# Attention scores of a head pair issued as one group, with two of their banks from the general PSUM pool

## The chip, the cores and the metric

The kernel runs on one NeuronCore of a Trainium2 chip, as one launch. The metric is the device time in microseconds of a whole execution. The median over 8 runs of the kernel before is 347.16 us (345.54 to 348.53).

A word on the engines as they are named here: PE is TensorE (PEld its weight loads), ACT is ScalarE, DVE is VectorE, POOL is GpSimd, SP is SyncE, which only issues transfers. [...]

## The reference

```python
def _attn_ref(q, k, v, f):                     # q, k, v: 8 x 8 x 576 x 64; f: 8 x 8 x 576
    scores = scale * np.matmul(q, k.transpose(0, 1, 3, 2))
    cum = np.cumsum(np.log(np.clip(f, 0.0001, 1.0)), axis=-1)
    decay = cum[:, :, :, None] - cum[:, :, None, :]
    scores = np.where(causal, -1000000000.0, scores + decay)
    attn = np.exp(scores - np.max(scores, axis=-1, keepdims=True))
    attn = attn / (np.sum(attn, axis=-1, keepdims=True) + 1e-09)
    return np.matmul(attn, v)

def _moe_ref(x, w_in, w_out):                  # x: 4608 x 512, w_in: 512 x 2048, w_out: 2048 x 512
    h = x @ w_in
    g = h * (1.0 / (1.0 + np.exp(-h)))
    return g @ w_out
```

The output of a causal attention with forgetting, 8 batches of 8 heads of 576 positions, its heads put side by side, goes through a two-layer block with SiLU (called MoE in the code). Inputs and output are float32.

## The kernel before

**Attention.** The first 128 positions of each batch are done ahead of the loop by other functions. The loop works on the other 448 positions, two heads at a time: a *pair* `n`, 32 of them, four to a batch. The decay is folded into the values (`convert_v` on POOL), so a probability is the exponential of the scaled score.

`scores(n, c)` does one of three chunks of a pair's scores (L445). The two heads lie in partitions 0 to 63 and 64 to 127, so each matmul uses 64 rows of PE, and the two heads' matmuls run beside each other, each into its own PSUM bank. A chunk gets a tile of two banks from the pool `psc` (two tiles, four banks). Chunk 0 holds the diagonal blocks, whose upper triangle DVE clears (L469). Chunk 1 holds the scores against the first key block. Chunk 2 holds what is left, and the rows of the last 64 queries. Chunks 0 and 1 take one exponential of 1024 columns each on ACT (L464), chunk 2 one of 256 (L464) and one of 640 (L476), whose last block DVE masks (L483).

`attend(n)` multiplies the probabilities with the values (28 small matmuls, `dn`, L507 and L516) and divides by the sum (L524, L525). `back(m)` turns the result of two pairs into the layout of the MoE input, on PE into a tile `tx` (L549) or, where `BY_DMA`, with two transposing transfers on SP's queue (L539, L543).

**MoE.** The rows of the MoE input come in 13 groups of up to 512 columns. `m1_chunk` makes one of 16 chunks of the hidden layer: four matmuls into a bank `hp` (L568), tanh on ACT (L576), and a multiply on DVE (L577) that reads `hp` again and writes `gt`. `m2_part` makes a quarter of an output tile: four matmuls into a bank `po` (L613), which stays open over four parts; after the fourth ACT copies it out (L623), and POOL's queue stores it later (L592).

**Banks.** The other four PSUM banks are the pool `pbig`. `hp`, `po`, `dn` and `tx` all take theirs from it, one at a time, in the order in which the program gave them back. A bank is given back by the last instruction that reads it: for `hp` the multiply on DVE.

**Order.** The order on every engine is the one in which the Python code emits instructions. `fill(us)` emits MoE pieces worth so many microseconds by a simple cost (columns / 2.4 ns), choosing between `m1_chunk` and `m2_part` in `step` so that the two keep pace. `slot(us, first)` calls `fill` and then issues the stores that were waiting. `behind()` is the MoE work that is ready and not yet emitted. The loop over `m` (two pairs each) is:

```python
        scores(n, 0)
        scores(n, 1)
        prepare(n)
        slot(piece, 2)
        # back(m - 1)
        scores(n, 2)
        scores(n + 1, 0)
        prepare(n + 1)
        slot(piece, 2)
        scores(n + 1, 1)
        scores(n + 1, 2)
        slot(piece, 2)
        attend(n)
        attend(n + 1)
        slot(min(3.5, max(0.8, behind() - LAG)) if m > 1 else 0.8, 1)
```

`prepare(n)` casts the q and k of pair `n + 2` on POOL, transposes them into `qkT` with a transfer on SP (L428), loads those of pair `n + 4`, and at some `n` loads and converts values of the next batch. After the loop only MoE work is left, some 59 us of it by `behind()`.

Of the kernel before, what the change touches and what calls it, by code (L numbers as in the profile page):

```python
# [8 lines left out]
ACT = mybir.ActivationFunctionType  # L9
ALU = mybir.AluOpType  # L10
FP32 = mybir.dt.float32
BF16 = mybir.dt.bfloat16
P = 128
# [5 lines left out]
def kernel(  # L19
# [10 lines left out]
    nc = tc.nc  # L30

    B, H, S, D = q.shape
# [5 lines left out]
    SM = 512  # L38
    ST = S - SM
    NM = SM // P  # L40
    NR = NM - 1
    RB = NR * P
# [9 lines left out]
    scale = 1.0 / float(D) ** 0.5  # L52
# [380 lines left out]
    T0 = P  # L433
# [8 lines left out]
    AT |= {(c, 0): SM + (c - 1) * P for c in range(1, NM)}  # L442
    AT |= {(2, 1): RB, (3, 1): SM + RB, (3, 2): 2 * SM}

    def scores(n, c):  # L445
        b, p = divmod(n, NP)
        if c == 0:
            us[n] = upool.tile([P, 2, UW], BF16, name="u", tag="u")
        u, ut = us[n], uts[n % 4]
        t = qkT[n]  # L450
        sc = psc.tile([P, 2, SM], FP32, name="sc", tag="sc")
        for kb, q0, q1, o in CHUNKS[c]:
            for i in range(2):
                r = slice(i * D, (i + 1) * D)
                if kb == 0:
                    kt = kT0[b][r, p, :]
                else:
                    k0 = RB if kb == NM else kb * P + RB
                    kt = t[r, k0 : k0 + P]
                nc.tensor.matmul(  # L460
                    sc[:, i, o : o + q1 - q0], lhsT=kt, rhs=t[r, q0:q1], start=True, stop=True
                )
        w = SM if c < 2 else T0
        nc.scalar.activation(  # L464
            out=u[:, :, c * SM : c * SM + w], in_=sc[:, :, 0:w], func=ACT.Exp, scale=scale
        )
        if c == 0:
            x = u[:, :, 0:RB].rearrange("p i (a t) -> p i a t", t=P)
            nc.vector.tensor_tensor(  # L469
                out=x,  # L470
                in0=x,
                in1=tri[:, None, None, :].to_broadcast([P, 2, NR, P]),
                op=ALU.mult,
            )
        if c == 2:
            nc.scalar.activation(  # L476
                out=ut[:, :, 0:3:2, :].rearrange("p k i t -> p i k t"),
                in_=sc[:, :, T0 : T0 + (NM + 1) * ST].rearrange("p i (k t) -> p i k t", t=ST),
                func=ACT.Exp,
                scale=scale,  # L480
            )
            x = ut[:, NM, 0:3:2, :]
            nc.vector.tensor_tensor(  # L483
                out=x, in0=x, in1=trit[:, None, :].to_broadcast([P, 2, ST]), op=ALU.mult
            )

    NGR = 2 * NR + 1

# [2 lines left out]
    def attend(n):  # L491
        b, p = divmod(n, NP)
        if p % 2 == 0:
            xqs[n // 2] = xqp.tile([P, NGR, 2, D], BF16, name="xr", tag="xr", bufs=3)
        xq = xqs[n // 2]
        u, ut = us.pop(n), uts[n % 4]
        dn = pbig.tile([P, NGR, D + 1], FP32, name="dn", tag="big")

        def vals(kb, i):
            h = head(p, i)  # L500
            return v0[b][:, h, :] if kb == 0 else vbf[b][:, kb - 1, h, :]

        for i in range(2):
            for c in range(1, NM):
                for kb in range(c + 1):
                    o = AT[c, kb]
                    nc.tensor.matmul(  # L507
                        dn[:, i * NR + c - 1, :],
                        lhsT=u[:, i, o : o + P],
                        rhs=vals(kb, i),  # L510
                        start=(kb == 0),
                        stop=(kb == c),
                    )
        for i in range(2):
            for kb in range(NM + 1):
                nc.tensor.matmul(  # L516
                    dn[:, NGR - 1, :],
                    lhsT=ut[:, kb, i : i + 2, :].rearrange("p i t -> p (i t)"),
                    rhs=vals(kb, i),
                    start=(i == 0 and kb == 0),  # L520
                    stop=(i == 1 and kb == NM),
                )
        rec = recp.tile([P, NGR], FP32, name="rec", tag="rec")
        nc.vector.reciprocal(out=rec[:, :], in_=dn[:, :, D])  # L524
        nc.vector.tensor_tensor(  # L525
            out=xq[:, :, p % 2, :],
            in0=dn[:, :, 0:D],
            in1=rec[:, :, None].to_broadcast([P, NGR, D]),
            op=ALU.mult,
        )  # L530
# [30 lines left out]
    def m1_chunk(g, fc):  # L561
        w = GW[g]
        if fc == 0:
            gts[g] = gpool.tile([P, NFC, w], BF16, name="gt", tag="gt")
        gt = gts[g]
        hp = pbig.tile([P, w], FP32, name="hp", tag="big")
        for cc in range(NCC):
            nc.tensor.matmul(  # L568
                hp[:, :],
                lhsT=w_in_bf[:, cc, fc * P : (fc + 1) * P],  # L570
                rhs=xcols(g, cc),
                start=(cc == 0),
                stop=(cc == NCC - 1),
            )
        th = tpool.tile([P, w], BF16, name="th", tag="th")
        nc.scalar.activation(out=th[:, :], in_=hp[:, :], func=ACT.Tanh, scale=0.5)  # L576
        nc.vector.scalar_tensor_tensor(  # L577
            out=gt[:, fc, :],
            in0=th[:, :],
            scalar=1.0,  # L580
            in1=hp[:, :],
            op0=ALU.add,
            op1=ALU.mult,
        )
# [4 lines left out]
    def store(n):  # L589
        n = max(n, 0)  # L590
        for q_, dst, src in stores[:n]:
            q_.dma_start(out=dst, in_=src)  # L592
        del stores[:n]
# [46 lines left out]
    def step():  # L640

        a, c = at["m1"], at["m2"]
        can1 = a < len(M1) and M1[a][0] in ready
        g1 = M1[a][0] if a < len(M1) else NG
        g2 = M2[c][0] if c < len(M2) else NG
        if can1 and M1[a][1] == 0 and g1 > g2 + 1:
            can1 = False
        can2 = open2["w"] and c < len(M2) and g2 < g1
        if not can1 and not can2:
            return None  # L650
        if can1 and can2:
            f1 = M1[a][1] / NFC
            f2 = (c - sum(M2_OF[:g2])) / M2_OF[g2]
            want = 3 - at["last"] if abs(f1 - f2) < 0.15 else (1 if f1 < f2 else 2)
            if want == at["last"] and at["row"] >= 2 and abs(f1 - f2) < 0.25:
                want = 3 - want
            if sum(M2_OF[: g2 + 1]) - c <= 2 and f1 >= 0.75:
                want = 1
            can1 = want == 1
        kind = 1 if can1 else 2  # L660
        at["row"] = at["row"] + 1 if kind == at["last"] else 1
        at["last"] = kind
        if can1:
            m1_chunk(*M1[a])
            at["m1"] += 1
            return 4 * (GW[g1] / 2.4 + 2.5)
        m2_part(*M2[c])
        at["m2"] += 1
        return 4 * (DM / 2.4 + 2.5)

    def behind():
        t = sum(4 * (GW[g] / 2.4 + 2.5) for g, _ in M1[at["m1"] :] if g in ready)
        t += sum(4 * (DM / 2.4 + 2.5) for g, _, _ in M2[at["m2"] :] if g in ready)
        return t / 1000

    def fill(us_, first=0, least=0):
        if first:
            at["last"], at["row"] = 3 - first, 2
        at["left"] += us_ * 1000
        while at["left"] > 0 or least > 0:  # L680
            t = step()
            if t is None:
                at["left"] = 0.0
                return False
            at["left"] -= t
            least -= 1
        return True
# [135 lines left out]
    def slot(us_, first=0):  # L823
        n = len(stores)
        fill(us_, first)
        store(n)
        for x in pending:
            x[0] -= 1
        while pending and pending[0][0] == 0:
            ready.update(pending.pop(0)[1])  # L830

    for m in range(NQ):
        n = 2 * m
        piece = 1.7 if m < 2 else 2.4
        scores(n, 0)
        scores(n, 1)
        prepare(n)
        slot(piece, 2)
        if m > 0:
            back(m - 1)  # L840
            if m % 2 == 0:
                b = m // 2 - 1
                pending.append([1 + BY_DMA[m - 1], [REST_OF[b]] + ([TAILS_OF[b][0]] if b == NM - 1 else [])])
        scores(n, 2)
        scores(n + 1, 0)
        prepare(n + 1)
        slot(piece, 2)
        scores(n + 1, 1)
        scores(n + 1, 2)
        slot(piece, 2)  # L850
        attend(n)
        attend(n + 1)
        slot(min(3.5, max(0.8, behind() - LAG)) if m > 1 else 0.8, 1)
    back(NQ - 1)
    ready.update([REST_OF[B - 1], TAILS_OF[B - 1][0]])
    for x in pending:
# [35 lines left out]
```

The softmax here doesn't subtract the row's maximum and nothing guards it: scores larger than these inputs give would overflow.

## Time and profile before

| | |
|---|---|
| median of 8 runs | 347.16 us (345.54 to 348.53) |
| the profiled execution | 345.54 us |
| its span, first to last instruction | 343.8 us |
| granted TensorE clock | 0.999 |
| first scores of the loop, last attend begins | 60.4 us, 275.7 us |
| ACT, DVE, POOL busy | 63%, 53%, 37% |

Times in the profile are microseconds from the start of the span. A row of the timeline has the start, the time until the end of the last of its instructions, the engine, the line, the operation, what it writes and reads, the shape and the count; in brackets stands how long the engine was idle before it and what ended that. A row of the waits has who waited for whom, and then total microseconds, times, and the longest. The ends of matmuls are modelled and overlap the next start, so PE's pace is read from start to start. A few matmul records are missing, so a count of `x3` can be four.

### The profile page before, as it was taken

What the parts mean: (1) busy time and instruction counts of PE and PEld (TensorE: products, weight loads), DVE (VectorE), ACT (ScalarE), POOL (GpSimd) and SP (SyncE); (2) the same over time, 40 slices, a digit from 0 to 9 for tenths busy, and PEclk for the clock granted to TensorE, in tenths of its full rate; (3) what the DMA queues carried; (4) which work ended last, traced back from release to release, by engine and by line L of the source; (5) the groups of instructions that cost most, each with busy time, mean ns of one, the idle gap of its engine ahead of it and who ended that gap; (6) DMA issues with size and microseconds to landing.
All of it is one profiled execution on the core that took longest, in us unless ns stands there. A gap on an engine that the chain in (4) does not pass through costs nothing.

```text
span 343.8 us, 8845 instructions
## 1 busy us (share of the span) xinstructions
PE 331.8 (97%) x3520; PEld 199.1 (58%) x3567; DVE 180.8 (53%) x389; ACT 218.1 (63%) x401; POOL 128.9 (37%) x227
## 2 busy tenths in 40 slices
PE   8999999989999999999999999999999999999995
PEld 3654656556656656466465665656656565555664
DVE  4766635455567456366545653547645454535330
ACT  5867555877687766757759667595775934444441
POOL 8895325833517354155137137126320000010011
PEclk9999999999999999999999999999999999999999
DMA  8999999999689998799899889779732000010013
GB/s 156 188 191 220 184 187 154 229 210 193 158 178 201 204 210 171 167 200 187 162 203 156 186 195 196 162 160 185 159 86 59 31 32 31 32 58 28 39 39 85
DMA packets 141497, 50.44 MB, mean 147 GB/s; under 512 B 132368, under 2 KB 138768, under 8 KB 141456
## 3 DMA queue, kind: packets, MB, share of 16 engines
q1 hardware_dynamic: 131440, 32.70, 52.8%
q0 software_dynamic: 9856, 17.04, 21.3%
q8 instruction: 28, 0.46, 0.6%
q10 hardware_dynamic: 160, 0.13, 0.1%
q14 instruction: 13, 0.11, 0.1%
HBM read 36.85 MB, written 9.44 MB: 135 GB/s over the span
## 4 chain that ended last, share of the span: by engine, by line
PE 74%; DMA 12%; SPq 5%; POOL 4%; issue 2%; DVE 1%; ACT 1%; POOLq 0%
PE po L613 30%; PE hp L568 29%; PE sc L460 6%; PE dn L507 4%; DMA w_out_bf<-in_moe_w_out_dram 3%; SPq L158 3%; DMA qktf<-in_k_dram 3%; DMA vf<-in_v_dram 2%; PE dn L516 2%; SPq L428 2%; DMA qkb<-in_k_dram 1%; DMA qkT<-qkb 1%; PE tp L286 1%; DMA kf<-in_k_dram 1%; SPq L168 1%
## 5 line engine op out<-in xcount | busy, mean ns | idle before, releaser
L576 ACT ACTIVATE th<-hp 128x384 bf16<-128x384 f32 (+2 forms) x208 | 96.0, 478 | 89.1 <-PE hp L568 85.3
L577 DVE SCALAR_TENSOR_TENSOR gt<-th,hp 128x384 bf16<-128x384 bf16 (+2 forms) x208 | 106.1, 522 | 80.6 <-ACT th L576 76.9
L613 PE MATMUL po<-w_out_bf,gt 128*128 128x512 bf16 (+1 forms) x550 | 137.6, 373 | 3.1 <-issue 1.4
L568 PE MATMUL hp<-x,w_in_bf 128*128 128x384 bf16 (+2 forms) x700 | 128.7, 321 | 0.5
L568 PEld LDWEIGHTS <-w_in_bf 128*128 128x128 bf16 x832 | 78.5, 98 | 55.2 <-issue 2.2
L613 PEld LDWEIGHTS <-gt 128*128 128x128 bf16 x592 | 54.6, 98 | 49.7 <-issue 2.1
L464 ACT ACTIVATE u<-sc 128x1024 bf16<-128x1024 f32 (+1 forms) x96 | 75.1, 821 | 12.0 <-PE sc L460 11.9
L592 POOL DMA_DIRECT2D out_dram<-osb x38 | 21.0, 553 | 131.3 <-ACT osb L623 88.3
L414 POOL TENSOR_TENSOR vp<-vf,w_bf 128x520 bf16<-128x520 f32 (+1 forms) x32 | 34.6, 1082 | 31.0 <-DMA vf<-in_v_dram 23.4
L469 DVE TENSOR_TENSOR u<-u,tri 128x768 bf16<-128x768 bf16 x32 | 21.7, 677 | 20.7 <-ACT u L464 20.7
L623 ACT ACTIVATE osb<-po 128x512 f32<-128x512 f32 (+1 forms) x37 | 22.0, 595 | 12.3 <-PE po L613 12.2
L400 POOL CAST qkb<-qf 128x384 bf16<-128x384 f32 x32 | 17.4, 545 | 32.6 <-DMA qf<-in_q_dram 31.6
L460 PE MATMUL sc<-qkT 64*128 64x128 bf16 (+1 forms) x640 | 26.5, 207 | 2.0 <-DMA qkT<-qkb 2.0
L483 DVE TENSOR_TENSOR ut<-ut,trit 128x128 bf16<-128x128 bf16 x32 | 8.5, 265 | 35.0 <-ACT ut L476 34.9
L460 PEld LDWEIGHTS <-qkT 64*128 64x128 bf16 x640 | 18.2, 94 | 13.1 <-issue 8.4
L476 ACT ACTIVATE ut<-sc 128x640 bf16<-128x640 f32 x32 | 23.3, 727 | 0.0
L507 PEld LDWEIGHTS <-u 128*128 128x128 bf16 x576 | 20.7, 97 | 2.5
L507 PE MATMUL dn<-vp,u 128*128 128x65 bf16 x384 | 21.8, 193 | 0.0
L525 DVE TENSOR_TENSOR xr<-dn,rec 128x448 bf16<-128x448 f32 x32 | 20.0, 624 | 1.1
L507 PE MATMUL dn<-v,u 128*128 128x65 bf16 x192 | 19.8, 193 | 0.0
L400 POOL CAST qkb<-kf 128x384 bf16<-128x384 f32 x32 | 16.4, 513 | 6.7 <-DMA kf<-in_k_dram 6.5
L568 PE MATMUL hp<-xt,w_in_bf 128*128 128x256 bf16 x128 | 18.2, 272 | 0.3 <-DVE gt L577 0.2
(68 smaller groups left out, 203.9 us busy)
## 6 DMA issues: line engine op xcount, KB each, us to landing
out_dram<-osb POOLq DMA_DIRECT2D x32, 256.0 KB, 3.1
vf<-in_v_dram SPq DMA_DIRECT2D x26, 256.0 KB, 5.0
qf<-in_q_dram SPq DMA_DIRECT2D x64, 96.0 KB, 2.9
kf<-in_k_dram SPq DMA_DIRECT2D x64, 96.0 KB, 2.9
w_in_bf<-in_moe_w_in_dram POOLq DMA_DIRECT2D x4, 512.0 KB, 7.2
w_out_bf<-in_moe_w_out_dram POOLq DMA_DIRECT2D x4, 512.0 KB, 9.3
vf<-in_v_dram POOLq DMA_DIRECT2D x6, 256.0 KB, 10.2
qkb<-in_q_dram POOLq DMA_DIRECT2D x8, 128.0 KB, 5.6
```

Source lines behind the costliest of these rows:

```text
L400: nc.gpsimd.tensor_copy(out=t2[:, c0 : c0 + NR, :].rearrange("p c x -> p (c x)"), in_=t[:, :, :, :].rearrange("p c h d -> p (c h d)"),)
L414: nc.gpsimd.tensor_tensor(out=vbf[b][r, c, :, :], in0=vst[b][c][r, :, :], in1=w_bf[r, c + 1, b * H : (b + 1) * H, None].to_broadcast([n, H ...
L460: nc.tensor.matmul(sc[:, i, o : o + q1 - q0], lhsT=kt, rhs=t[r, q0:q1], start=True, stop=True)
L464: nc.scalar.activation(out=u[:, :, c * SM : c * SM + w], in_=sc[:, :, 0:w], func=ACT.Exp, scale=scale)
L469: nc.vector.tensor_tensor(out=x, in0=x, in1=tri[:, None, None, :].to_broadcast([P, 2, NR, P]), op=ALU.mult,)
L476: nc.scalar.activation(out=ut[:, :, 0:3:2, :].rearrange("p k i t -> p i k t"), in_=sc[:, :, T0 : T0 + (NM + 1) * ST].rearrange("p i (k t) ...
L507: nc.tensor.matmul(dn[:, i * NR + c - 1, :], lhsT=u[:, i, o : o + P], rhs=vals(kb, i), start=(kb == 0), stop=(kb == c),)
L568: nc.tensor.matmul(hp[:, :], lhsT=w_in_bf[:, cc, fc * P : (fc + 1) * P], rhs=xcols(g, cc), start=(cc == 0), stop=(cc == NCC - 1),)
L576: nc.scalar.activation(out=th[:, :], in_=hp[:, :], func=ACT.Tanh, scale=0.5)
L577: nc.vector.scalar_tensor_tensor(out=gt[:, fc, :], in0=th[:, :], scalar=1.0, in1=hp[:, :], op0=ALU.add, op1=ALU.mult,)
L613: nc.tensor.matmul(po[:, :], lhsT=gt[:, fc, tb * P : (tb + 1) * P], rhs=w_out_bf[:, fc, m0:m1], start=(fc == 0), stop=(fc == NFC - 1),)
L623: nc.scalar.activation(out=osb[:, :], in_=po[:, :], func=ACT.Copy, scale=0.5)
```

## The change

- `scores(n)` now issues all three chunks of a pair one after the other.
- Chunks 0 and 2 still take tiles of `psc`. Chunk 1 takes two single banks of `pbig`, one for each head, and its exponential is split into one of 512 columns for each bank.
- The two exponentials of chunk 2, and the mask after them, are kept back in a list `late`. They are emitted behind the next `m1_chunk`, or at the end of the slot if it emits none.
- The loop has two score groups for each `m` instead of three, with longer slots between them, and a short slot between the two attends.

```diff
-    def scores(n, c):
+    late: list = []
+    def scores(n):
         b, p = divmod(n, NP)
-        if c == 0:
-            us[n] = upool.tile([P, 2, UW], BF16, name="u", tag="u")
+        us[n] = upool.tile([P, 2, UW], BF16, name="u", tag="u")
         u, ut = us[n], uts[n % 4]
         t = qkT[n]
-        sc = psc.tile([P, 2, SM], FP32, name="sc", tag="sc")
-        for kb, q0, q1, o in CHUNKS[c]:
...
+        sc = {}
+        for c in range(3):
+            if c == 1:
+                sc[c] = [pbig.tile([P, SM], FP32, name="sb", tag="big") for _ in range(2)]
+            else:
+                sc[c] = psc.tile([P, 2, SM], FP32, name="sc", tag="sc")
+            for kb, q0, q1, o in CHUNKS[c]:
...
+            if c == 0:
+                nc.scalar.activation(
+                    out=u[:, :, 0:SM], in_=sc[c][:, :, :], func=ACT.Exp, scale=scale
                 )
...
+            if c == 1:
+                for i in range(2):
+                    nc.scalar.activation(
+                        out=u[:, i, SM : 2 * SM], in_=sc[c][i][:, :], func=ACT.Exp, scale=scale
+                    )
+        def rest():
+            x = sc[2]
+            nc.scalar.activation(
+                out=u[:, :, 2 * SM : UW], in_=x[:, :, 0:T0], func=ACT.Exp, scale=scale
+            )
...
+        late.append(rest)

         if can1:
             m1_chunk(*M1[a])
+            while late:
+                late.pop(0)()

     def slot(us_, first=0):
         n = len(stores)
         fill(us_, first)
+        while late:
+            late.pop(0)()
         store(n)

-        piece = 1.7 if m < 2 else 2.4
-        scores(n, 0)
-        scores(n, 1)
+        piece = 2.2 if m < 2 else 3.4
+        scores(n)
         prepare(n)
         slot(piece, 2)
...
-        scores(n, 2)
-        scores(n + 1, 0)
+        scores(n + 1)
         prepare(n + 1)
         slot(piece, 2)
-        scores(n + 1, 1)
-        scores(n + 1, 2)
-        slot(piece, 2)
         attend(n)
+        slot(0.7, 1)
         attend(n + 1)
-        slot(min(3.5, max(0.8, behind() - LAG)) if m > 1 else 0.8, 1)
+        slot(min(3.0, max(0.6, behind() - LAG)) if m > 1 else 0.6, 1)
```

More of the change, by code (lines that the diff above doesn't have):

```diff
@@ L443 @@
     AT |= {(2, 1): RB, (3, 1): SM + RB, (3, 2): 2 * SM}
-    def scores(n, c):
+    late: list = []
+    def scores(n):
         b, p = divmod(n, NP)
-        if c == 0:
-            us[n] = upool.tile([P, 2, UW], BF16, name="u", tag="u")
+        us[n] = upool.tile([P, 2, UW], BF16, name="u", tag="u")
         u, ut = us[n], uts[n % 4]
         t = qkT[n]
-        sc = psc.tile([P, 2, SM], FP32, name="sc", tag="sc")
-        for kb, q0, q1, o in CHUNKS[c]:
[L453 to L461, printed above, removed]
-                )
[L463 to L473, printed above, removed]
@@ new lines, in scores @@
+        sc = {}
[6 more added lines that the diff above has]
+                for i in range(2):
+                    r = slice(i * D, (i + 1) * D)
+                    if kb == 0:
+                        kt = kT0[b][r, p, :]
+                    else:
+                        k0 = RB if kb == NM else kb * P + RB
+                        kt = t[r, k0 : k0 + P]
+                    x = sc[c][i] if c == 1 else sc[c][:, i, :]
+                    nc.tensor.matmul(
+                        x[:, o : o + q1 - q0], lhsT=kt, rhs=t[r, q0:q1], start=True, stop=True
+                    )
+            if c == 0:
+                nc.scalar.activation(
+                    out=u[:, :, 0:SM], in_=sc[c][:, :, :], func=ACT.Exp, scale=scale
+                )
+                x = u[:, :, 0:RB].rearrange("p i (a t) -> p i a t", t=P)
+                nc.vector.tensor_tensor(
+                    out=x,
+                    in0=x,
+                    in1=tri[:, None, None, :].to_broadcast([P, 2, NR, P]),
+                    op=ALU.mult,
+                )
+            if c == 1:
+                for i in range(2):
+                    nc.scalar.activation(
+                        out=u[:, i, SM : 2 * SM], in_=sc[c][i][:, :], func=ACT.Exp, scale=scale
+                    )
@@ L474, in scores @@
+        def rest():
+            x = sc[2]
+            nc.scalar.activation(
+                out=u[:, :, 2 * SM : UW], in_=x[:, :, 0:T0], func=ACT.Exp, scale=scale
             )
-        if c == 2:
             nc.scalar.activation(
                 out=ut[:, :, 0:3:2, :].rearrange("p k i t -> p i k t"),
-                in_=sc[:, :, T0 : T0 + (NM + 1) * ST].rearrange("p i (k t) -> p i k t", t=ST),
+                in_=x[:, :, T0 : T0 + (NM + 1) * ST].rearrange("p i (k t) -> p i k t", t=ST),
```

## The prediction

> **What bounds the kernel now.** I read the page's busy row first, then the waits of TensorE (PE), then the timeline of one stretch, then the groups by form.
>
> ```profile
> span 343.8 us, 8845 instructions
> PE 331.8 (97%) x3520; PEld 199.1 (58%) x3567; DVE 180.8 (53%) x389; ACT 218.1 (63%) x401; POOL 128.9 (37%) x227
> ```
> ```profile
> PE sc L460 <- DMA qkT<-qkb: 2.0, 2, 1.5
> ...
> PE hp L568 <- DVE gt L577: 0.2, 1, 0.2
> ```
>
> PE is busy 97%, and its waits in the whole kernel add up to about 5 us. A busy row alone could hide slack, so I checked start times: four `hp` matmuls of 384 columns take 0.65 us and four `po` matmuls 0.86 us, start to start. That is columns / 2.4 per ns, plus 2 ns each, at a granted clock of 0.999. From the first scores to the end PE streams at its peak. So the kernel time is PE's work plus PE's waits. The change can only pay by taking something from PE, and it costs whatever it makes PE wait. Two things besides matmuls are on PE's path:
>
> ```profile
> 59.89 0.60 PE L568 MATMUL hp<-x,w_in_bf 128*128 128x256 bf16 x4
> 60.42 0.40 PE L460 MATMUL sc<-qkT 64*128 64x128 bf16 x8
> 60.66 0.33 PE L460 MATMUL sc<-qkT,kT 64*128 64x384 bf16 x2
> 60.82 0.22 PE L460 MATMUL sc<-qkT 64*128 64x128 bf16 x2
> 60.97 1.90 PE L613 MATMUL po<-w_out_bf,gt 128*128 128x512 bf16 x8
> ```
>
> First, the step into and out of the scores. The four 256-column matmuls need 0.43 us and are through at 60.32; the scores start at 60.42. The last score pair (128 columns, 0.05 us) is through at 60.87; `po` starts at 60.97. So each step costs 0.10 us, and over all groups of the trace the start times give 0.095 to 0.099.
>
> ```profile
> 190.12 0.81 PE L568 MATMUL hp<-x,w_in_bf 128*128 128x384 bf16 x4
> 190.97 0.49 ACT L576 ACTIVATE th<-hp 128x384 bf16<-128x384 f32 x1 [2.45 <-PE hp L568]
> 191.49 0.56 DVE L577 SCALAR_TENSOR_TENSOR gt<-th,hp 128x384 bf16<-128x384 bf16 x1 [0.30 <-ACT th L576]
> ```
> ```profile
> 215.60 1.47 PE L568 MATMUL hp<-xt,w_in_bf 128*128 128x256 bf16 x12
> 215.82 0.71 ACT L476 ACTIVATE ut<-sc 128x640 bf16<-128x640 f32 x1
> 216.40 1.09 ACT L576 ACTIVATE th<-hp 128x256 bf16<-128x256 f32 x3
> 216.84 1.11 DVE L577 SCALAR_TENSOR_TENSOR gt<-th,hp 128x256 bf16<-128x256 bf16 x3
> 217.31 0.60 PE L568 MATMUL hp<-xt,w_in_bf 128*128 128x256 bf16 x4 [0.24 <-DVE gt L577]
> ```
>
> Second, the return of a PSUM bank of `pbig`. An `hp` chunk is through at 190.76; tanh starts 0.20 later, takes 0.49, the multiply starts 0.03 later and ends at 192.05. The bank is back 1.29 us after the last column, 1.34 with the hop to PE (217.26 to 217.31). The second fence is the only place where this decides now: four `hp` chunks in a row behind scores whose exponentials hold ACT, and the fourth waits (0.40 us between start times, against columns / 2.4). `pbig` has four banks; an open `po` holds one, so `hp` turns over in three.
>
> **The change part by part.**
>
> *Fewer score groups.* Scores stand in three groups per query step `m` before and in two after: 16 groups fewer, 32 steps fewer. The row says 0.097 us each: 3.1 us off PE. The Trainium skill, TensorEngine Tiling (Array Packing), Key Properties, says that changing the tiling mode drains TensorE, without a price; TensorE: Matmul & The Clock Gate, Step-by-step: what each phase is for, puts the drain of the array at some 128 cycles, 0.053 us by estimate, which would make it 1.7 us. I take the row: **-3.1**.
>
> *The later second score group.* Before the `scores` of pair `n+1`, PE now does 2.2 (later 3.4) us of pieces instead of 1.7 (2.4). In `m` = 1 and 2 the scores waited for `qkT` (1.70 and 0.58 between start times, the transposes landing at 74.76 and 85.89). SP's order (transposes, loads, `back`'s transposes) and POOL's (casts, then stores per slot) is the same sequence as before, so I keep the landings. PE arrives later, also because of the waits below; about 0.4 is left: **-1.9**. From `m` = 3 on the transposes land microseconds ahead.
>
> *Two banks of `pbig` per pair.* `c`=1 takes two banks at once, in order of return, and with an open `po` that is the second- and third-last `hp`'s. Let T be the end of the last `hp` before the scores. `c`=1 wants its banks at T+0.34 (step 0.10, chunk 0 0.24); without waits the group ends at T+0.89 (chunks 0.21 and 0.24, step 0.10).
> - If two `hp` stand directly before the scores, the earlier one's tanh runs T-0.45 to T+0.04, its multiply to T+0.63, and its bank is back at T+0.69: wait 0.35.
> - If an `hp` follows directly, it wants the last `hp`'s bank, back at T+1.34: wait 0.45, or 0.10 if 0.35 was waited already.
> - If a second `hp` follows, it wants the first score bank. ACT: exponential of chunk 0 from T+0.57; next start 0.90 later (1.93 us for a pair of such rows, 1.03 the last); the 512-wide one ends at T+2.07, bank back 2.13, PE there at T+1.99: wait 0.15.
>
> I wrote out the planner's order of `hp`, `po`, scores and attends for all `m` and put each group into its class:
> - two before, two behind, `po` open (pairs 8, 12, 16, 20): 0.61 each, 2.4;
> - one directly before, one behind (10, 14): 0.45 each, 0.9;
> - two before, a `po` part behind (26): 0.35;
> - three `hp` behind the moved exponentials of the pair before (27, 31): those hold ACT 0.85 just ahead of three tanh, so both banks come late: 0.27 + 0.47, 0.04 behind: 0.8 each, 1.6;
> - pairs 7 and 18, and attend 23 (its `dn` needs a bank after two `hp`): 0.5, 0.5, 0.2.
> That is 6.45 in `m` = 3 to 15. The other groups stand next to `po` parts (0.86 us without a new bank) and wait for nothing. In `m` = 1 and 2 the same rules give 1.7 (`back` through PE also takes a bank).
>
> *Chunk 2's exponentials behind the next piece.* The move takes two ACTIVATEs and one DVE multiply past a tanh (or a `po` eviction) and its multiply; it issues no DMA. What queues behind: the next tanh, counted above. Who waits: `attend(n)`, a slot later and covered by over 3 us of pieces; where `po` parts alone fill the slot (pairs 13, 17) `attend` comes right behind, still about level. And pair 1: it is pair 0's late release of `psc`, where the exponentials are the last thing ACT gets before scores 1: 1.0 us. So `m` = 0 to 2 pay 2.75 in bank waits.
>
> *Split exponential.* Two 512-wide ones instead of one of 1024: 0.48 each start to start against 0.90, +0.05 per pair. The Trainium skill, ScalarE: Activation LUTs, Rules for kernel authors, budgets about 0.3 us per ACTIVATE plus 0.83 ns per element; by that the first score bank comes 0.13 later and the split costs ACT 0.3 per pair: about +0.8 us in the sum, estimated from the pairs that wait for that bank. The rows stand back to back here, so I take +0.05, already in the walk. ACT at 63% bears 32 x 0.05.
>
> *Slot sizes, attends apart.* MoE work per `m` shrinks by 0.2 us and runs after the loop, where PE is as dense; 0. If `attend` were late here nothing else would cover it, at most 0.3 us in some six steps; a gain from standing apart is excluded, since attends wait for nothing now. I take 0, and keep +1.8 for the range.
>
> Sum: waits 2.75 + 6.45 - 0.40 (the one removed at 217.3) = +8.8; -1.9; -3.1; **+3.8 us**. The profiled execution took 345.5 (span 343.8 and 1.7 around it), which gives 349.3; the median of the runs shown is 1.6 above it, so **351.0**.
>
> **The rivals.**
> - *Faster: the saved steps decide.* If banks come back sooner than in my walk (another order of handing out, ACT ahead), only the -3.1 and -1.9 remain. The point is the sum of bank waits in the score groups: below 5.4 us (mine is 9.2) the change gains. At 3 us the sum is -2.4, **344.8**. For it: before, bank waits are only 0.4 us. Against: before, scores took no bank of `pbig`, and 217.3 shows what one `hp` too many does.
> - *Much slower: waits chain.* If every group waits like 27 and 31 (0.8 x 32 = 26, less those counted), or late exponentials hold the attends, it is +8 to +15, **358**. Against: `po` parts stand next to half of the groups and let ACT catch up.
> - *The change doesn't do what it says.* The slot without a free `hp` flushes the exponentials only at its end (pairs 9, 13, 17), and steps saved could return elsewhere; then waits and gains are both smaller, about **347.5**.
>
> **How the numbers follow.** My sum: 0.70 (slower). Much slower: 0.09. Faster: 0.14. Not doing what it says: 0.07, of which most is no change. 0.3% (1.0 us) is about what a measurement of this kernel can tell. Faster 0.15, same 0.06, slower 0.79. The range 346.3 to 355.5 takes in the unknowns of my sum (bank waits 2 us either way, 1.8 for attends), the no-change case and the near part of the others.
>
> **What would show it.** PE waits at L460 and L568 ended by DVE `gt` and ACT `u`, tens of them, each under 0.6 us, some 6 to 9 us together; one of about 1 us early for ACT `ut`; `qkT` waits below 1 us. Chunk exponentials 32 x 1024, 64 x 512, 32 x 256. Steps in and out of scores: 64 in the loop. I am wrong if PE's waits stay near 5 us in all, or if attends (L507, L516) wait for more than 1 us.

## The result, and the profile after

The changed kernel takes 351.29 us (median of 11 runs, 349.79 to 353.35), against 346.86 us for the kernel before over the runs made beside it. The ratio is 1.0126, with a 95% interval of 1.0107 to 1.0145: **1.3% slower**. The forecast was 351.0 us and slower. The profiled execution took 350.08 us, against 345.54 before.

The first lines to read are again the span, PE's busy row and PE's waits:

```profile
span 348.3 us, 8873 instructions
...
PE 334.6 (96%) x3516; PEld 203.4 (58%) x3567; DVE 186.3 (53%) x389; ACT 220.7 (63%) x433; POOL 129.6 (37%) x227
```
```profile
PE hp L588 <- DVE gt L597: 1.3, 3, 0.5
PE wm L232 <- DVE warm L204: 1.2, 1, 1.2
PE sc L469 <- ACT ut L494: 0.8, 1, 0.8
PE sc L469 <- DMA qkT<-qkb: 0.5, 1, 0.5
PE po L633 <- issue: 0.5, 3, 0.2
PE hp L588 <- ACT u L485: 0.3, 1, 0.3
```

The span grew by 4.5 us. Yet these waits still add up to about 5 us, as before, and PE still looks 96% busy: its busy time even grew by 2.8 us, with the same matmuls. (About 0.9 of these come from the records: a missing one shows as idle time with "issue" beside it, 0.5 us here and 1.4 us before.) The end of a matmul record is modelled. It lies later than the time at which the next matmul can start (a 384-column row lasts about 0.33 us and streams for 0.16), so a wait shorter than that tail counts as busy. It shows only between start times. Here is one score group, that of pair 8, in the timeline of the changed kernel, with the chunks ahead of it and behind it:

```profile
108.53 1.46 PE L588 MATMUL hp<-x,w_in_bf 128*128 128x384 bf16 x8
109.90 1.20 DVE L597 SCALAR_TENSOR_TENSOR gt<-th,hp 128x384 bf16<-128x384 bf16 x2 [0.18 <-ACT th L596]
109.92 0.40 PE L469 MATMUL sc<-qkT 64*128 64x128 bf16 x8
110.16 0.67 PE L469 MATMUL sb<-qkT,kT 64*128 64x384 bf16 x2
110.41 1.02 ACT L473 ACTIVATE u<-sc 128x1024 bf16<-128x1024 f32 x1
110.51 0.23 PE L469 MATMUL sb<-qkT 64*128 64x128 bf16 x1
...
111.15 1.63 PE L588 MATMUL hp<-x,w_in_bf 128*128 128x384 bf16 x8
111.32 1.09 ACT L485 ACTIVATE u<-sb 128x512 bf16<-128x512 f32 x2
```

No row carries an idle time for PE, but there are three waits. The two heads' 384-column matmuls normally start together and last 0.33 us. Here they last 0.67: the second head's bank is still being read by a multiply on DVE (the first of the two in the second row, 109.90 to 110.45), and its matmul waits 0.34. The group ends late, and the next `hp` starts 0.14 late, on the bank of the last `hp`, which the second multiply reads until 111.10. Then eight `hp` matmuls take 1.63 us where 1.46 is usual (the first row, for instance): the fifth waits 0.17 for the first score bank, which the first of the two exponentials of L485 gives back. The working for two chunks before and two behind had 0.35, 0.10 and 0.15.

The largest waits for `pbig` stand at the score groups of pairs 27 and 31, where three `hp` follow the exponentials that were moved, and both banks come late. For pair 27 the timeline has the two rows together for 0.78 us:

```profile
244.12 0.40 PE L469 MATMUL sc<-qkT 64*128 64x128 bf16 x8
244.63 0.78 PE L469 MATMUL sb<-qkT,kT 64*128 64x384 bf16 x2
245.10 0.23 PE L469 MATMUL sb<-qkT 64*128 64x128 bf16 x1
```

The first `sb` should start 0.24 after the group, at 244.36, and starts at 244.63. The second head's stands behind it until shortly before 245.10. The group loses 0.74 us. The one long wait of its kind that the waits do show is at pair 1, for `psc`:

```profile
63.48 0.33 PE L469 MATMUL sb<-qkT,kT 64*128 64x384 bf16 x2
63.64 0.22 PE L469 MATMUL sb<-qkT 64*128 64x128 bf16 x2
64.71 0.23 PE L469 MATMUL sc<-qkT 64*128 64x128 bf16 x2 [0.85 <-ACT ut L494]
```

All of it, read from PE's start times (next start less columns / 2.4, and less the usual length of a score group), for the profiled executions:

| | before | after | forecast for after |
|---|---|---|---|
| score groups; one `m`'s groups with their steps | 48; 1.90 us | 32; 1.69 us | |
| saved by fewer steps | | 3.3 us | 3.1 us |
| waits for `qkT` | 2.3 us | 0.55 us | 0.4 us |
| waits for banks, inside and behind score groups | 0.5 us | 10.4 us | 9.2 us |

The differences are -3.3, -1.75 and +9.9, or +4.85 us; the span grew by 4.5.

### The profile page after: what moved, and what is told of

Same layout as the page of the kernel before. It is cut to its first block, busy times and chain, and to the rows that moved or that the text cites. A ratio compares the mean times of both kernels' runs of the same rounds, so it can differ in the third digit from the quotient of the medians.

```text
span 348.3 us, 8873 instructions
## 1 busy us (share of the span) xinstructions
PE 334.6 (96%) x3516; PEld 203.4 (58%) x3567; DVE 186.3 (53%) x389; ACT 220.7 (63%) x433; POOL 129.6 (37%) x227
## 4 chain that ended last, share of the span: by engine, by line
PE 82%; ACT 6%; DVE 5%; DMA 3%; issue 3%; POOL 1%
PE po L633 33%; PE hp L588 32%; PE dn L527 4%; PE sc L469 3%; DVE gt L597 3%; PE dn L536 2%; ACT th L596 2%; PE tp L286 2%; DMA qkT<-qkb 2%; PE sb L469 1%; DMA f_sb<-in_f_dram 1%; PE sc L320 1%; ACT u L485 1%; ACT u L473 1%; ACT x L391 1%
## 5 line engine op out<-in xcount | busy, mean ns | idle before, releaser
L597 DVE SCALAR_TENSOR_TENSOR gt<-th,hp 128x384 bf16<-128x384 bf16 (+2 forms) x208 | 107.6, 523 | 91.8 <-ACT th L596 88.3
L596 ACT ACTIVATE th<-hp 128x384 bf16<-128x384 f32 (+2 forms) x208 | 98.2, 479 | 89.4 <-PE hp L588 87.5
L633 PE MATMUL po<-w_out_bf,gt 128*128 128x512 bf16 (+1 forms) x546 | 136.2, 373 | 2.6 <-issue 0.5
L588 PE MATMUL hp<-x,w_in_bf 128*128 128x384 bf16 (+2 forms) x700 | 130.6, 321 | 2.8 <-DVE gt L597 1.3
L633 PEld LDWEIGHTS <-gt 128*128 128x128 bf16 x592 | 56.0, 98 | 48.6
L473 ACT ACTIVATE u<-sc 128x1024 bf16<-128x1024 f32 x32 | 32.9, 1027 | 8.7 <-PE sc L469 8.6
L485 ACT ACTIVATE u<-sb 128x512 bf16<-128x512 f32 x64 | 35.0, 611 | 0.0
L469 PEld LDWEIGHTS <-qkT 64*128 64x128 bf16 x640 | 20.0, 94 | 16.1 <-issue 12.8
L501 DVE TENSOR_TENSOR ut<-ut,trit 128x128 bf16<-128x128 bf16 x32 | 11.0, 344 | 19.5 <-ACT ut L494 19.5
L400 POOL CAST qkb<-kf 128x384 bf16<-128x384 f32 x32 | 17.5, 546 | 6.0 <-DMA kf<-in_k_dram 5.9
```

What stands on the lines that cost most here:

```text
L400: nc.gpsimd.tensor_copy(out=t2[:, c0 : c0 + NR, :].rearrange("p c x -> p (c x)"), in_=t[:, :, :, :].rearrange("p c h d -> p (c h d)"),)
L469: nc.tensor.matmul(x[:, o : o + q1 - q0], lhsT=kt, rhs=t[r, q0:q1], start=True, stop=True)
L473: nc.scalar.activation(out=u[:, :, 0:SM], in_=sc[c][:, :, :], func=ACT.Exp, scale=scale)
L485: nc.scalar.activation(out=u[:, i, SM : 2 * SM], in_=sc[c][i][:, :], func=ACT.Exp, scale=scale)
L588: nc.tensor.matmul(hp[:, :], lhsT=w_in_bf[:, cc, fc * P : (fc + 1) * P], rhs=xcols(g, cc), start=(cc == 0), stop=(cc == NCC - 1),)
L597: nc.vector.scalar_tensor_tensor(out=gt[:, fc, :], in0=th[:, :], scalar=1.0, in1=hp[:, :], op0=ALU.add, op1=ALU.mult,)
```

## The experiments

The theory is the prediction's: the time goes to PE waiting for `pbig` banks, because each score group takes two at once. The rivals are the split exponential, the moved exponentials, and the order of slots and attends. Ratios are against the kernel before, each with its 95% interval.

**One bank instead of two.** Chunk 1's matmuls of the second head are left out, and both exponentials read the first head's bank.

```diff
-                sc[c] = [pbig.tile([P, SM], FP32, name="sb", tag="big") for _ in range(2)]
+                sc[c] = [pbig.tile([P, SM], FP32, name="sb", tag="big")] * 2
...
-                for i in range(2):
+                for i in range(1 if c == 1 else 2):
```

> The changed kernel, but chunk 1 takes one bank of pbig for both heads: the second head's chunk-1 matmuls are left out (they ran beside the first head's, so PE's time stays) and both 512-wide exponentials read the one bank. Steps into and out of the scores, ACT's and DVE's work and the order stay. Theory (the two banks make PE wait): the waits of PE within and just behind the score groups fall from about 7.3 us to about 2.5, the scores' first matmul into sb waits in at most two or three groups, and the time comes out about 1 us below the kernel before, ratio 0.995 to 1.000. Rival (the split exponential, the moved exponentials or the slot sizes cost the time): nothing of that is changed, so the ratio stays near 1.0126.

Measured: 345.64 us, ratio 0.996 (0.9944 to 0.9976). The span fell from 348.3 to 343.9. The same pair 8:

```profile
108.36 1.46 PE L588 MATMUL hp<-x,w_in_bf 128*128 128x384 bf16 x8
109.75 0.40 PE L469 MATMUL sc<-qkT 64*128 64x128 bf16 x8
109.99 0.32 PE L469 MATMUL sb<-qkT,kT 64*128 64x384 bf16 x1
...
110.50 1.47 PE L588 MATMUL hp<-x,w_in_bf 128*128 128x384 bf16 x8
```

From the group's start to the next `hp` it is 0.75 us, against 1.23, and eight `hp` take 1.47 again. The matmuls left out are no gain in themselves: a score group that waits for nothing takes 0.75 us in the changed kernel as well. The merged order, the two exponentials of 512 and the moved ones are all still there; the second bank alone turned a gain of 0.4% into a loss of 1.3%. The waits left were about 6 us, not the 2.5 that I named beside the ratio: the 1.0 us at pair 1 stays, and some of the waits at `hp`, `dn` and `tx` do.

**The banks without the gain.** The kernel before in its own order, with chunk 1 in two `pbig` banks and two exponentials.

```diff
+        if c == 1:
+            sc = [pbig.tile([P, SM], FP32, name="sb", tag="big") for _ in range(2)]
+        else:
+            sc = psc.tile([P, 2, SM], FP32, name="sc", tag="sc")
...
+        for i in range(2 if c == 1 else 0):
+            nc.scalar.activation(
+                out=u[:, i, SM : 2 * SM], in_=sc[i][:, :], func=ACT.Exp, scale=scale
+            )
...
```

> The kernel before, in its own order with three score groups per m, but chunk 1 takes two banks of pbig and its exponential is split into two of 512. No step into the scores is saved and nothing is moved. Theory (the two banks): the waits appear alone, without the gain; as chunk 1 is now followed by hp pieces sooner and each m has two such groups, 8 to 10 us slower than the kernel before, ratio 1.023 to 1.03, with PE waits at the sb matmuls and at hp. Rival (the merged order or the moved exponentials cost the time, banks are free enough): only the split exponential is left, at most 1.6 us of ACT that nothing waits for, ratio 1.000 to 1.003.

Measured: 356.83 us, ratio 1.0293 (1.0246 to 1.0341), in the expected range. Even the view of the waits has some of it:

```profile
PE hp L577 <- DVE gt L586: 2.8, 7, 0.6
PE sb L464 <- DVE gt L586: 2.2, 5, 0.9
```

**The split alone.** The kernel before, chunk 1 in `psc`, its exponential in two.

```diff
+        for i in range(2 if c == 1 else 0):
+            nc.scalar.activation(
+                out=u[:, i, SM : 2 * SM], in_=sc[:, i, :], func=ACT.Exp, scale=scale
+            )
+        if c != 1:
...
```

> The kernel before with chunk 1 in its psc tile as it was, but its exponential of 1024 columns split into two of 512. Theory (ACT bears the split, banks are the cost): ACT has 0.05 us more per pair and nothing waits for it, ratio 0.998 to 1.003. Rival (the split exponential is a good part of what the kernel with sb banks in the old order lost): 0.3 us more per pair on ACT[...], ratio 1.008 or more.

Measured: 347.28 us, ratio 1.0013 (0.9996 to 1.003). So of the 2.9% of the experiment before, the split is at most 0.3%, and it may be nothing. By form, ACT has

```profile
L465 ACT ACTIVATE u<-sc 128x512 bf16<-128x512 f32 x64 | 35.2, 613 | 6.7 <-PE sc L460 6.6
L469 ACT ACTIVATE u<-sc 128x1024 bf16<-128x1024 f32 x32 | 33.2, 1038 | 3.9 <-PE sc L460 3.9
```

64 rows with 35.2 us of busy time cover what 32 of 33.2 do: 0.06 per pair.

**The exponentials at once.** The changed kernel with chunk 2's exponentials ahead of the next tanh.

```diff
-        late.append(rest)
+        rest()
```

> The changed kernel with chunk 2's exponentials emitted at once, ahead of the next tanh, instead of behind the next piece. Theory (banks come back too late): the next tanh now stands behind 0.85 us more of ACT work, so the hp bank and the hp banks after it come back later; PE's waits at hp rise by 5 to 6 us, the 1.0 us wait for psc at pair 1 and the double waits at pairs 27 and 31 get smaller, in all about 4 us slower than the changed kernel, ratio about 1.023. Rival (the moved exponentials themselves cost the time): the kernel gets about 2 to 3 us faster than the changed one, ratio about 1.005.

Measured: 355.56 us, ratio 1.0254 (1.0201 to 1.0307), 4.3 us above the changed kernel. Putting them behind the next piece is worth about 1.3%, though it costs the wait at pair 1 and a third of those at 27 and 31. In PE's start times the wait at pair 1 falls from 1.0 us to 0.1 and those inside the groups of 27 and 31 from 0.74 to 0.49 each; the waits outside the score groups go from about 3 us to about 8. The longest is the last of these rows of the waits:

```profile
PE hp L588 <- DVE gt L597: 2.6, 6, 0.6
...
PE hp L588 <- ACT osb L643: 1.0, 1, 1.0
```

**One more group.** The kernel before with four score groups per `m`.

```diff
         scores(n, 2)
+        fill(piece / 2, 2)
         scores(n + 1, 0)
         prepare(n + 1)
-        slot(piece, 2)
+        slot(piece / 2, 2)
```

> The kernel before with one more score group per m: half of the second slot's pieces stand between chunk 2 of pair n and chunk 0 of pair n+1. 16 groups more, so 32 steps more. Theory (0.097 us for each step, whatever stands around it): +3.1 us, less up to 1 us because the scores of pair 3 and 5 come later and wait less for their transposes: ratio 1.006 to 1.009. [...]+1.7 less the same: ratio 1.002 to 1.005.

Measured: 348.94 us, ratio 1.0061 (1.0032 to 1.0091). The interval alone does not exclude the smaller price, the 1.7 us for 32 steps of the prediction's estimate. The timeline does:

```profile
154.76 0.98 PE L568 MATMUL hp<-x,w_in_bf 128*128 128x384 bf16 x5
155.67 0.23 PE L460 MATMUL sc<-qkT 64*128 64x128 bf16 x2
155.73 0.19 PE L460 MATMUL sc<-qkT,kT 64*128 64x64 bf16 x2
155.76 0.28 PE L460 MATMUL sc<-qkT 64*128 64x64 bf16 x8
155.97 1.04 PE L613 MATMUL po<-w_out_bf,gt 128*128 128x512 bf16 x4
```

Five `hp` matmuls take 0.81 us, so they are through at 155.57, and the scores start at 155.67. The groups of one `m` take 2.10 us against 1.90 before: 0.20 for one more group, 0.10 for each step, whichever matmuls stand around it. 3.3 us more of this, and 1.8 less waiting for `qkT`, leave 1.5; the ratio says 2.1 (1.1 to 3.2).

**The attends together.** The changed kernel without the 0.7 us slot between the attends.

```diff
         attend(n)
-        slot(0.7, 1)
+        fill(0.0)
+        for x in pending:
+            x[0] -= 1
+        while pending and pending[0][0] == 0:
+            ready.update(pending.pop(0)[1])
         attend(n + 1)
```

> The changed kernel without the 0.7 us slot between the two attends; its pieces go into the later slots of the same and the next m (the change of readiness that the slot brought is kept). The prediction took standing apart as worth 0 and named at most 1.8 us. Theory (banks of pbig): each attend takes a bank too, dn comes back 1.1 us after its last matmul, and two of them in a row ahead of hp pieces take two of three banks; the walk through the order gives about 2.3 us slower than the changed kernel, ratio 1.017 to 1.021, with more waits at hp. Rival (the attends do not bear on the banks, only their own inputs count): within 0.7 us of the changed kernel, ratio 1.011 to 1.0145.

Measured: 353.09 us, ratio 1.0165 (1.0137 to 1.0194). It is 1.8 us above the changed kernel by the medians and 1.4 by the ratios, whose intervals overlap a little. That lies between the two expectations, and banks are the smaller part of it. In PE's start times of the profiled executions the waits for banks grew by only 0.6 us. Those for `qkT` grew by 1.4, as the scores come earlier in the order. Another 0.8 us is attend 9 (121.15 to 122.42 in the timeline), which waits for its own chunk 2: the moved exponentials and their mask are not done when it follows attend 8 at once. So the rival, that an attend's own inputs count, has a part in it too:

```profile
PE sc L469 <- DMA qkT<-qkb: 1.8, 2, 1.4
...
PE dn L536 <- DVE ut L501: 0.3, 1, 0.3
```

**A version that is faster than both.** The kernel before, with the pieces of `m` = 1 and 2 shared out otherwise, so that PE comes to the first scores of pairs 3 and 5 when their transposes have landed.

```diff
         piece = 1.7 if m < 2 else 2.4
+        own = {1: (2.2, 1.7, 1.2), 2: (3.4, 1.7, 2.1)}.get(m, (piece,) * 3)
...
-        slot(piece, 2)
+        slot(own[0], 2)
...
```

(The second and third slot take `own[1]` and `own[2]`.)

> The kernel before with the pieces of m = 1 and 2 shared out otherwise: slots of 2.2, 1.7, 1.2 and 3.4, 1.7, 2.1 us, so that PE comes to the first scores of pairs 3 and 5 later, when their transposes have landed; the sum per m stays. Theory (those two waits of 2.3 us belong to PE's place in the order, not to the transfers' work): the waits for qkT fall to about 0.5 us and the time by 1 to 2 us, ratio 0.995 to 0.998. Rival (the transposes follow PE's progress and land later as well): ratio 0.999 to 1.001.

Measured: 345.49 us, ratio 0.9956 (0.9934 to 0.9977); the span is 342.3. The waits have what was expected:

```profile
PE sc L460 <- DMA qkT<-qkb: 0.2, 1, 0.2
```

By start times it is 0.4 us where it was 2.3. So the 1.75 us that the change gained at `qkT`, which need no bank, can be had by moving work within two steps of the loop.

## Why the prediction was right

- **Fewer steps, -3.1 us.** -3.3 measured. Shown: 0.20 us per group saved in the changed kernel and the same per group added with four groups. The row decided over the estimate from the Trainium skill (TensorE: Matmul & The Clock Gate, Step-by-step: what each phase is for: 0.053 us per drain, -1.7).
- **`qkT`, -1.9 us.** -1.75 measured. That these waits hang on PE's place in the order and not on the transfers is shown by the last experiment.
- **Bank waits, +8.8 us.** +9.9 measured. The classes stand as worked out: pairs 8, 12, 16 and 20 lose 0.65 each (0.61 forecast), 10 and 14 0.49 (0.45), 26 0.35 (0.35), 27 and 31 0.77 (0.78), pair 1 1.0 (1.0), `m` = 1 and 2 1.95 (1.7; with pair 1 the prediction's parts make 2.7, where it carried on 2.75). One wait was not foreseen, 0.64 us for an `hp` after attend 24; it is told below.
- **The split exponential, +0.05 per pair.** ACT has 0.06 more per pair, and alone it costs the kernel at most 0.3%. The 0.3 per pair, the prediction's other estimate, did not come. The 0.3 us per ACTIVATE behind it (Trainium skill, ScalarE: Activation LUTs, Rules for kernel authors) is given there for a bias passed as a `[128,1]` operand, and these exponentials have no bias.
- **Attends apart, taken as 0.** Here the step was wrong in its reason: I excluded a gain because attends waited for nothing before. In the changed order, standing apart is worth about 1.4 us, through `qkT` and the attend's own inputs more than through banks. The sum did not suffer, since the walk followed the real order with the slot in it.
- **What would show it.** I expected tens of PE waits in the view of the waits, and named waits that "stay near 5 us in all" as a sign of error. They did stay there, and the forecast held all the same: that sign was badly chosen, because waits under the modelled tail of a matmul do not appear in that view.
- **The rivals.** The faster case had its point at 5.4 us of bank waits; the experiment with one bank had about 6 us of them. Its profiled span is that of the kernel before (343.9 against 343.8), its ratio 0.996: the turning point lies about there. The much slower case did not come, as 18 of the 32 score groups wait for no bank. Nor did the case in which the change doesn't do what it says: the trace has 32 score groups, and 64 exponentials of 512 columns.
- **The number itself.** That it came within 0.3 us is in part luck. The medians grew by 4.4 us where +3.8 was forecast, and the forecast started from eight runs of the kernel before, whose median was 0.3 us above that of all 32.

## What to carry to other kernels

Where one engine is at its peak, a buffer taken from a pool that others turn over has to be priced in the time it takes to come back: write down the order of allocations, give each its return time from the rows, and add up who comes too early. Read waits of TensorE from start to start; neither its busy share nor a list of idle times shows those shorter than the tail of a record. Before merging work to save such steps, look whether the pool has the banks for it, and whether part of the gain can be had by order alone.

## What the runs showed of the hardware

I had not expected the wait after attend 24, nor the slow mask that leads to it. DVE's small mask (L501) usually takes 0.226 us. In the changed kernel it stood at this place:

```profile
233.36 1.13 DVE L501 TENSOR_TENSOR ut<-ut,trit 128x128 bf16<-128x128 bf16 x1 [0.32 <-ACT ut L494]
234.41 1.00 DVE L597 SCALAR_TENSOR_TENSOR gt<-th,hp 128x384 bf16<-128x384 bf16 x2
```
```profile
233.45 0.52 POOL L400 CAST qkb<-qf 128x384 bf16<-128x384 f32 x1
233.89 0.51 POOL L400 CAST qkb<-kf 128x384 bf16<-128x384 f32 x1
```

The mask lasts until POOL's casts from SBUF are nearly through. The multiplies behind it come late, and the `hp` that wants their bank waits 0.64 us. Of the 13 masks that POOL's casts or multiplies overlap in the changed kernel, all are slower than 0.25 us, six of them at 0.5 to 0.8 and this one at 1.13; the 19 others take 0.224 to 0.226. In the kernel before five of eight such are slower. The split experiment, which leaves the mask where it was before, has one of 1.44 us beside POOL's casts and multiplies, at a place where the kernel before has 0.38:

```profile
106.43 1.44 DVE L488 TENSOR_TENSOR ut<-ut,trit 128x128 bf16<-128x128 bf16 x1 [1.30 <-ACT ut L481]
```

The next attend then waits 1.1 us for a bank, where it waited 0.06. So a good part of the 1.6 us between these two profiled spans (345.4 and 343.8) lies behind this one mask. The Trainium skill, SBUF — State Buffer, Who interferes with whom, says that a DVE instruction with two SBUF inputs contends with a GpSimd instruction that reads SBUF; the rows fit it, though no run here took POOL's work away to test it, so the cause of the slow masks is not shown. The move of chunk 2's mask past another piece should have been looked at against POOL's casts, too.
